# A spectral layer and a top-1 expert layer on one core: the order of the steps up to the main part, written anew

## The chip, the core and the metric

The kernel runs on one core of a Trainium2 chip. The metric is the device time of one execution in microseconds (us), the median of several runs. Engines are named as in the profile: PE does matmuls, PEld is its weight loading, DVE, ACT and POOL are the elementwise engines, SP only issues transfers. Indirect DMAs (gathers and scatters) are issued from POOL.

## The reference, cut to what matters

```python
X = np.fft.rfft(x, axis=1)                       # x: 8 x 1856 x 256
Yr = Xr @ w_r - Xi @ w_i + b_r
Yi = Xr @ w_i + Xi @ w_r + b_i
Yr = np.sign(Yr) * np.maximum(np.abs(Yr) - 0.01, 0.0)   # Yi likewise
y = np.fft.irfft(Yr + 1j * Yi, n=1856, axis=1)   # its 14848 rows go to the experts
g_idx = np.argmax(x @ w_group, axis=1)           # 4 groups
e_idx = np.argmax(xg @ w_expert[g], axis=1)      # 4 experts in each
h = np.maximum(xg[mask_e] @ w1[g, e], 0.0)       # 256 -> 1024
ye = h @ w2[g, e]                                # 1024 -> 256
out[tok_idx] = g_w * e_w * ye                    # product of both softmax values
```

Every row goes through one of 16 experts. So the rows have to be routed (a softmax and an argmax over groups, then over the experts of that group) and sorted by expert before the expert matmuls can take them in blocks.

## The kernel before

The sequences are worked on in 4 pairs. Each pair's transform is made of small steps, and so is all that follows. A step is a Python generator's piece up to its next `yield`; it issues the instructions of mostly one engine. Each kind of step has a letter: `e` is the second forward transform (PE, L760), `h` the low part of its result (DVE, L782), `y` and `k` the complex linear layer (PE, L824 and L827, then L842), `z` its share from DVE (L832) between the two, `q` the low part of its input (POOL, L808), `r` and `v` the inverse transform (PE, L866 and L884), `x` its turn (DVE, L905), `G` and `H` the gate's logits (PE, L916, and DVE, L925).

A pair's rows are routed and sorted in two halves, so there are 8 halves, here numbered first to eighth. For each half:

- `R`, 30 steps, is the route: a chain on DVE (L176 to L255) with softmax exponentials on ACT, row numbers on POOL (L218), two matmuls that count the rows per expert (L228 and L230, into a tile `bank` of PSUM), then `runs` on POOL (L236 to L240), `first_run` on DVE (L241) and the place of every row, of which L250 reads the two counts out of `bank` again.
- `S`, 11 steps, is the sort: `at`, `to` and `step` on POOL (L265 to L277), the goal on DVE (L279 to L283), `run` and `place` on POOL (L286 to L291), and then twice, for each part of the half, `in_run` (L298, L301), `here` (L304, L306) and `what` (L309), all on POOL.
- `N`, 3 steps, is PE's side of it: L325 for each part, from `in_run` and `what`, and L331 for both. `O` copies the results out (ACT, L340).
- `P` scatters the sorted row numbers into the list `lst` in DRAM (POOL, L346).

`in_run`, `here` and `what` have one buffer each, so the second part's L298 waits for the first part's L325. The pool of `bank` has 3 buffers and serves nearly all matmuls of the head: a step that takes a bank waits until the step that had it has been read out.

Once enough rows are sorted, 8 early expert jobs run beside the rest of the head, from a list a and a list b: `I` reads the list (SP, L956 and L959), `Z` converts it (POOL, L353 to L358), `F` gathers rows (POOL, L542, two gathers a step), `T` turns them (PE, L981), `U` and `D` are the two expert matmuls (PE, L1002; L1025 and L1027), `J` adds the halves (DVE, L1043) and `K` stores the rows by an indirect DMA (POOL, L624). `M` at the end gathers the first rows of the main part, which begins with L560 and L577 at about 491 us and has an order of its own.

What sets the order in the head is the string `ORDER` alone, 1702 letters: the loop at L1099 calls `next()` on the step that each letter names. Every engine runs its own instructions in the order in which the string issues them; between engines there are only the semaphores for data and for buffers. An engine that waits holds up all that stands behind it in its queue, DMAs on POOL's queue too.

Of the kernel before, what the change touches and what calls it, by code (L numbers as in the profile page):

```python
# [43 lines left out]


ORDER = """
ccQddccQdQddddjdcccddddddcddQejQffhheQiigegfcyhQQQQyfzikzhiggddkmpomcjoqcfdyjfzhiyzhkkiddggemocpdmoqdjfjlcyydfzhizkhgimk
gdpdemeofhcoqfjdjiyyzhkzgklimgdepomjofhjiqcdyzyfkhzigkgpqmdmoojfjchefiyyzkhizggdpmdkmojefofjqhyhyzzigikgpmqokfjehfyihzke
gimgpojmofhqyzjfihgykizmgpkmfoojqrsfjyyshhiziggrsskmpzrkeomfqfssohrhjsyijiyggcsdcvzwdxklwcxdmdddczvpvddqxkowwxxcmvjddlww
xywxxwecffozjdhGhdiiggHRvvpRxcwRRxxRyRwqdRkzRwxkRdvwmmRovRwxxjRxcowRReRwxyjyRzRfRkzwRRRdmhkdiRoRRigRgRGRjmfehpqRoyHRRRRR  # L50
zjfSShfyhiRzSkiggRRSRkmRpmqeojoefRfyjhyzRighkiRzSRRRRRkeRSmgpRRfRoRRqjShyigzRigmRpqoRfkjmfhNORyfojShhSSryzigigRpskmsrRzk
SmoNOjsqsrosjseyfhzNOfyilzhRrsksiPmggkvompwxxoqejwvwjvfxyxywwfzxvkwzkhmhxwxxiwcdlodgmijgGpoRSSSSSSSNOvHRqxRwvxRxSSSjcwdd
yywRzRRxvewRfxRzfRcddkwhhwkimiRxRgRRglSNOvcxwxweRRRRpmdqodfRolhfGRRjNORihjyRziRRgykgzRHRpkPmmefRofqRRRRoRhRcjdhjicRSSSRy
yzgRzRSkiddRkmgSpeRdmoqSfSfRocRjhlRNOjiRchygyRzidzgdpdkkdmqRomeRjffRRSoyRRRzhRSRhjiRgiSkemRffgRoRyrSjhhiizggNOksrymsojNO
ysRzsRPrsskmezfrohfjhsskWimgWiyloWWgzvvwxxxjwwVwvxxkevVymoVwVjyzfwRSSSSSSSfhkzxNOSShiwxmxSiwogkgmefSfjohhigNOGviygwHvNOR
xRRRxRwRzRxPRwjxRvwRwkmRxRoRjRwRexWIRRvywyWzRxRRkRWRmzRxRRRRRRlkomfGhiiojjRSSSSZygHgRzRRykRRRfFweRVmffheWzkRohRRRjhyziRm
iRgoRjSkgRRfSyTRRfRhziSRkhNOSmojmRRVRygiogjyzRzkRSSRmSRRoVkmNOoXrYsVrsRFsNOPsUrlAUsBsrWUssVWWAVvwRSSSSSSxSvxvwNOxSBwSxUx
vwwwxVwTDxxwXAYGHBSvWWwWRSxNOAvWxRRRURRBxRVRADRUwNOPwRvlxwBRRAUwIZxBRRARRvFUFDDxVVWWRRxVWRAVEBBwVEVRwDwxDJRWRRRRKRDRRRTE
DXYFEURJKJUATBlSSSAUJBWUGAASBFVXYHSTSWDSUBDANOWRWSVRKWUARVSBURBRSlRDRRRRVRRDUXEATAYSVRDRFBRUBVJERRWVWRVDRKWJNONORRERARBU
URRRAPDBFAUKRRRBDWXVYDlUABUAJTVABBDDEEKUAUBWJDDWAXYUBWVVWAEJUKKJADEBVBRSSSSSSSNOSSSJDDUTSNOEVJUAXDYABUNOAPBDBDUUAAKEKBBU  # L60
DDAJBDEEKKLDDKJMJKEJKK
"""

_OFF = {}
# [1424 lines left out]
```

## Time and profile before

| | us |
|---|---|
| median of 3 runs | 1113.06 (1109.84 to 1118.94) |
| the profiled execution | 1116.01 |
| its span | 1114.2 |
| PE busy in the span | 1047.2 (94%) |
| DVE busy | 675.2 (61%) |
| ACT busy | 489.9 (44%) |
| POOL busy | 426.5 (38%) |

The profiled execution is 2.95 us above the median, and 1.8 us of it lie around the span. Its mean granted clock of PE is 0.98 of full speed. How to read it: PE's share of 94% is a mean over a head in which it waits at many places and a main part in which it nearly doesn't; so the times by stretch matter more than the shares. An engine's idle time counts only where the chain of waits goes through it.

### The profile page before, as it was taken

How to read it: one execution, taken by the hardware profiler on the slowest of the kernel's cores; microseconds unless marked ns; L12 is line 12 of the kernel's file. 1: busy time of each engine (PE TensorE's matmuls, PEld its weight loads, DVE VectorE, ACT ScalarE, POOL GpSimd, SP SyncE). 2: the span in 40 equal slices, each digit the busy share in tenths (PEclk: the TensorE clock that was granted, in tenths of full speed). 3: DMA queues.
4: the chain of work that ended last, by engine and by line, in shares of the span. 5: the costliest groups of instructions: out<-in, count | busy, mean ns of one | idle time of the engine just before them, and what ended most of it. 6: DMA issues, size and time to landing. Idle time of an engine off the chain costs nothing.

```text
span 1114.2 us, 24634 instructions
## 1 busy us (share of the span) xinstructions
PE 1047.2 (94%) x9688; PEld 908.8 (82%) x9688; DVE 675.2 (61%) x1599; ACT 489.9 (44%) x1273; POOL 426.5 (38%) x599
## 2 busy tenths in 40 slices
PE   8899989979888889799999999999999999999996
PEld 4685767756665678789899999999999999999996
DVE  6779988989688656336544564546545455545532
ACT  2464555544533423224443553435535445444532
POOL 0121163453356264564334333434334433432422
PEclk9999989999999989899999999999999999999999
DMA  9802502421303422022313321313223233133110
GB/s 382 192 3 87 218 2 78 154 78 59 116 30 110 166 91 77 6 84 103 120 43 124 126 100 50 132 37 125 75 80 129 58 110 117 55 112 111 43 35 28
DMA packets 35047, 107.08 MB, mean 96 GB/s; under 512 B 13628, under 2 KB 16153, under 8 KB 28402
## 3 DMA queue, kind: packets, MB, share of 16 engines
q1 hardware_dynamic: 18130, 57.75, 15.7%
q0 software_dynamic: 11904, 30.74, 8.6%
q10 hardware_dynamic: 4896, 17.01, 3.9%
q8 instruction: 77, 1.26, 0.5%
q14 instruction: 40, 0.33, 0.1%
HBM read 71.34 MB, written 34.28 MB: 95 GB/s over the span
## 4 chain that ended last, share of the span: by engine, by line
PE 74%; DVE 13%; issue 5%; POOL 4%; DMA 2%; ACT 1%; POOLq 0%; SPq 0%; ACTq 0%; DVEq 0%
PE ph L577 25%; PE py L650 13%; PE py L651 6%; PE py L672 6%; PE pw L842 5%; PE bank L866 3%; PE pw L824 2%; PE pg L560 2%; PE bank L760 2%; PE ph L1002 2%; DVE big L438 2%; PE bank L916 2%; DVE yt L905 2%; PE bank L434 2%; PE bank L884 1%
## 5 line engine op out<-in xcount | busy, mean ns | idle before, releaser
L577 PE MATMUL ph<-xth,big 128*128 128x256 f32 (+8 forms) x1280 | 293.7, 313 | 2.5 <-DVE hl L584 1.6
L584 DVE SCALAR_TENSOR_TENSOR hl<-ph,hh 128x256 fp32r<-128x256 f32 (+8 forms) x528 | 169.1, 356 | 113.1 <-ACT hh L582 98.0
L577 PEld LDWEIGHTS ph<-xth,big 128*128 128x128 f32 x1280 | 218.7, 190 | 5.8 <-PE ph L577 2.2
L650 PE MATMUL py<-big,hh 128*128 128x512 f32 (+2 forms) x608 | 218.9, 400 | 0.0
L582 ACT ACTIVATE hh<-ph 128x256 fp32r<-128x256 f32 (+8 forms) x528 | 153.4, 338 | 106.9 <-PE ph L577 94.4
L577 PE MATMUL ph<-xtl,big 128*128 128x256 f32 (+8 forms) x640 | 199.2, 311 | 0.4 <-DVE xtl L565 0.4
L542 POOL DMA_INDIRECT xg<-ys_d,gi_r x92 | 91.3, 993 | 246.6 <-PE pg L560 227.4
L651 PE MATMUL py<-big,hl 128*128 128x256 f32 (+2 forms) x608 | 171.3, 282 | 0.0
L650 PEld LDWEIGHTS py<-big,hh 128*128 128x128 f32 (+2 forms) x608 | 113.0, 186 | 27.0 <-DVE yo L691 0.3
L624 POOL DMA_INDIRECT out_dram<-yo,si_r x92 | 91.6, 996 | 91.5 <-DVE yo L656 39.6
L577 PEld LDWEIGHTS ph<-xtl,big 128*128 128x128 f32 x640 | 121.6, 190 | 0.7 <-DVE xtl L565 0.6
L651 PEld LDWEIGHTS py<-big,hl 128*128 128x128 f32 (+2 forms) x608 | 113.3, 186 | 0.5 <-issue 0.3
L656 DVE SCALAR_TENSOR_TENSOR yo<-py,ent_r,yo 128x256 f32<-128x256 f32 (+1 forms) x66 | 31.9, 484 | 133.5 <-ACT yo L655 118.7
L655 ACT ACTIVATE yo<-py,ent_r 128x256 f32<-128x256 f32 (+1 forms) x66 | 31.3, 474 | 149.0 <-PE py L651 85.8
L672 PE MATMUL py<-hh,big 128*128 128x320 f32 (+4 forms) x320 | 75.4, 315 | 0.0
L808 POOL TENSOR_TENSOR xdl<-xd,xdh 128x512 fp32r<-128x512 f32 (+1 forms) x23 | 28.1, 1221 | 116.6 <-ACT xdh L801 88.2
L524 DVE TENSOR_TENSOR big<-xt,big 128x512 fp32r<-128x512 f32 x104 | 71.2, 684 | 1.0 <-ACT big L523 0.2
L842 PE MATMUL pw<-wh,xh 128*128 128x256 f32 x240 | 66.5, 299 | 5.0 <-DVE pw L832 4.9
L523 ACT CAST big<-xt 128x512 fp32r<-128x512 f32 x104 | 65.5, 630 | 0.0
L842 PE MATMUL pw<-wl,xh 128*128 128x256 f32 x240 | 62.4, 282 | 0.0
L847 ACT ACTIVATE big<-pw,nlam 128x512 f32<-128x512 f32 x60 | 41.3, 688 | 41.5 <-PE pw L842 40.0
L842 PEld LDWEIGHTS pw<-wh,xh 128*128 128x128 f32 x240 | 45.5, 190 | 15.9 <-DVE pw L832 8.5
(247 smaller groups left out, 2024.5 us busy)
## 6 DMA issues: line engine op xcount, KB each, us to landing
xt<-in_w_dram SPq DMA_DIRECT2D x34, 1024.0 KB
ys_d<-ysb ACTq DMA_DIRECT2D x32, 512.0 KB
big<-in_x_dram SPq DMA_DIRECT2D x8, 1024.0 KB
xt<-in_x_dram SPq DMA_DIRECT2D x8, 1024.0 KB
lst<-L SPq DMA_DIRECT2D x1, 1936.0 KB
xg<-ys_d,gi_r POOLq DMA_INDIRECT x92
out_dram<-yo,si_r POOLq DMA_INDIRECT x92
CI<-in_cst_dram SPq DMA_DIRECT2D x1, 1088.0 KB
```

What stands on the lines that cost most here:

```text
L523: nc.scalar.copy(out=wt[:, 2 * i, cs], in_=raws[i][:, cs])
L524: nc.vector.tensor_tensor(out=wt[:, 2 * i + 1, cs], in0=raws[i][:, cs], in1=wt[:, 2 * i, cs].bitcast(F32), op=ALU.subtract)
L542: ins = nc.gpsimd.indirect_dma_start(out=xg[0:m, c, :], out_offset=None, in_=ys_d[0:rows, :], in_offset=bass.IndirectOffsetOnAxis(ap=ids.g ...
L577: nc.tensor.matmul(o[:, :n], lhsT=a_[:, ch, fs], rhs=b_[:, ch, 0:n], start=k == 0, stop=k == 5)
L582: nc.scalar.activation(out=hh[:, f, cs], in_=o[:, cs], func=AF.Relu)
L584: nc.vector.scalar_tensor_tensor(out=hl[:, f, cs], in0=o[:, cs], scalar=0.0, in1=hh[:, f, cs].bitcast(F32), op0=ALU.max, op1=ALU.subtract)
L624: ins = nc.gpsimd.indirect_dma_start(out=out, out_offset=bass.IndirectOffsetOnAxis(ap=ids.si[0:ids.rows(t), t:t + 1], axis=0), in_=ysb, in ...
L650: nc.tensor.matmul(o, lhsT=hh[:, f, ts], rhs=w2b[:, :, f, :], start=f == 0, stop=f == 7, skip_group_check=True)
L651: nc.tensor.matmul(o[:, 0:D], lhsT=hl[:, f, ts], rhs=w2h[:, f, :], start=False, stop=f == 7, skip_group_check=True)
L672: nc.tensor.matmul(o, lhsT=w_[:, f, ds_], rhs=h_[:, f, 0:n], start=f == 0 and h_ is hh and w_ is w2h, stop=f == 7 and h_ is hh and w_ is n ...
L842: ins = nc.tensor.matmul(y, lhsT=a_[:, h, k % 2, j], rhs=t[:, j, h], start=False, stop=a_ is xl and h == 1, skip_group_check=True)
L847: nc.scalar.activation(out=z_of(pr)[:, k], in_=psum["m", pr, k], func=AF.Relu, bias=nlam)
```

## The change

The string `ORDER` is replaced by another one with the same number of each letter. Steps, tiles, buffers and the main part are the same lines as before. Of its 15 lines the first one before and the first one now are:

```diff
 ORDER = """
-ccQddccQdQddddjdcccddddddcddQejQffhheQiigegfcyhQQQQyfzikzhiggddkmpomcjoqcfdyjfzhiyzhkkiddggemocpdmoqdjfjlcyydfzhizkhgimk
...
+cdcjdcddQdcjcdddddcdQdQcddcddQeiQeiggcQQfhfyQhyeQQzkfizfighmdiihgdokgpcmqejofgjdyfypzdikgzhhkimmocgopjqefjdhyizydkzfmhko
...
 """
```

What it moves shows on the engines. First PE at the fourth half's sort matmuls, L325 twice and L331. `what` and `in_run` come from POOL; the other rows are steps of the transform. Before:

```order
L325 MATMUL bank<-in_run,what 64x80 x8
...
L842 MATMUL pw<-wh,xl 128x256 x2
L760 MATMUL bank<-T,big 64x2x32 x32
L325 MATMUL bank<-in_run,what 64x80 x8
L916 MATMUL bank<-yt,wg 64x256 x32
L884 MATMUL bank<-big,CI 64x256 x8
L827 MATMUL pw<-wc,xd 128x256 x2
L884 MATMUL bank<-big,CI 64x256 x8
L331 MATMUL bank<-K,by_place 80x64 x2
```

Now, the first piece with the first L325, the second with the other two:

```order
L325 MATMUL bank<-in_run,what 64x80 x8
L827 MATMUL pw<-wc,xd 128x256 x2
L760 MATMUL bank<-T,big 64x2x32 x32
L916 MATMUL bank<-yt,wg 64x256 x32
L884 MATMUL bank<-big,CI 64x256 x8
L827 MATMUL pw<-wc,xd 128x256 x2
...
L760 MATMUL bank<-T,big 64x2x32 x32
L884 MATMUL bank<-big,CI 64x256 x8
L325 MATMUL bank<-in_run,what 64x80 x8
L827 MATMUL pw<-wc,xd 128x256 x4
L331 MATMUL bank<-K,by_place 80x64 x2
```

Before, two `k` steps (L842, the lines left out are theirs) and one `e` step (L760) stand between the two L325. Now the gate's L916, parts of `v` (L884), of `y` (L827) and two `e` steps stand there, and four `k` steps where the second piece has its line of dots.

Second, PE at the first turn of rows gathered from list b (L981), near the seventh half's route matmuls. Before:

```order
L228 LDWEIGHTS sl
L228 MATMUL bank<-oh,sl 128x256
L230 LDWEIGHTS ones
L230 MATMUL bank<-oh,ones 128x256
L1025 MATMUL bank<-big,hh 128x512
L1027 MATMUL bank<-big,hl 128x256
L1025 MATMUL bank<-big,hh 128x512
L1027 MATMUL bank<-big,hl 128x256
...
L981 MATMUL bank<-K,xg 128x128 x4
```

Now:

```order
L1025 MATMUL bank<-big,hh 128x512
L1027 MATMUL bank<-big,hl 128x256
L981 MATMUL bank<-K,xg 128x128 x4
L1025 MATMUL bank<-big,hh 128x512
L1027 MATMUL bank<-big,hl 128x256
...
L1002 MATMUL ph<-xth,big 128x256
L228 LDWEIGHTS sl
L228 MATMUL bank<-oh,sl 128x256
```

The turn stood behind the route matmuls of that half and now stands before them, with one `D` step (four pairs of L1025 and L1027) and one `U` step (L1002) between.

Third, POOL at the last half, where the second route (`runs`, `first_run`) and the sort (from L265 on) meet the stores of the expert jobs (L624). Before:

```order
L238 TENSOR_SCALAR runs<-runs 128x16
L240 MEMSET first_run 128x1
L346 DMA lst<-by_run,goal_i 7828x64
L542 DMA xg<-ys_d,gi_b 128x256 x2
L624 DMA out_dram<-yo,si_b 16384x256 x4
L265 MEMSET at 128x1
L266 MEMSET at 128x1
L268 TENSOR_SCALAR to<-first_run 128x16
L269 TENSOR_TENSOR at<-to,base 128x16
```

Now:

```order
L624 DMA out_dram<-yo,si_b 16384x256
L298 TENSOR_TENSOR in_run<-K,run 128x640
L301 TENSOR_SCALAR in_run<-in_run 128x640
L304 TENSOR_TENSOR here<-K,place 128x256
L306 TENSOR_SCALAR here<-here 128x256
L236 TENSOR_SCALAR runs<-cnt 128x16
...
L309 TENSOR_TENSOR what<-here,ent 128x512
L624 DMA out_dram<-yo,si_b 16384x256 x2
L265 MEMSET at 128x1
L266 MEMSET at 128x1
```

Four stores stood between `first_run` and the sort of the last half; now the last `what` of the seventh half and two stores do, while the eighth half's `runs` stands behind four sort operations of the seventh.

## Rows read from the trace of the kernel before

**Rows 1.** Stretches: us, length; busy (instructions) PE, PEld, DVE, ACT, POOL; clock; DMA; GB/s
```profile
0.00:134.00 134.00, 124.14 (x1854) 90.53 (x1858) 107.50 (x204) 65.94 (x139) 17.02 (x22) 0.97 0.54 180
134.00:167.00 33.00, 27.71 (x446) 22.04 (x444) 26.50 (x69) 16.25 (x38) 20.37 (x35) 0.90 0.04 14
...
215.00:253.00 38.00, 30.58 (x464) 23.41 (x463) 31.45 (x80) 16.56 (x41) 19.41 (x34) 1.00 0.22 78
253.00:286.00 33.00, 29.25 (x483) 21.23 (x485) 27.38 (x46) 16.86 (x37) 14.36 (x22) 0.98 0.17 66
286.00:375.00 89.00, 77.43 (x976) 55.23 (x976) 66.96 (x144) 36.47 (x82) 37.96 (x64) 0.97 0.25 85
375.00:398.00 23.00, 16.93 (x104) 14.11 (x105) 14.40 (x33) 7.95 (x17) 11.34 (x22) 0.85 0.60 203
...
450.00:470.00 20.00, 14.99 (x111) 13.34 (x111) 6.70 (x14) 3.48 (x9) 14.60 (x19) 0.83 0.02 8
470.00:491.00 21.00, 18.97 (x123) 16.31 (x122) 6.34 (x12) 5.69 (x12) 10.53 (x15) 1.00 0.18 52
491.00:1114.20 623.20, 610.95 (x3924) 574.94 (x3924) 314.83 (x857) 275.29 (x805) 233.80 (x304) 0.99 0.27 87
sum 1114.20, PE 1047.19 PEld 908.77 DVE 675.15 ACT 489.92 POOL 426.55; mean PE 95.20 PEld 82.62 DVE 61.38 ACT 44.54 POOL 38.78
```

**Rows 2.** Waits of PE, 0 to 491 us: total, times, longest
```profile
PE bank L325 <- POOL what L309: 11.8, 4, 5.0
PE bank L981 <- DVE t L250: 6.0, 1, 6.0
PE pw L842 <- DVE pw L832: 4.9, 8, 1.1
...
PE bank L325 <- DVE xl L782: 3.4, 1, 3.4
PE bank L228 <- DVE oh L222: 2.2, 1, 2.2
PE bank L916 <- DVE t L250: 1.8, 1, 1.8
```

**Rows 3.** Chain of waits, fourth half's sort: start, us, what
```profile
278.64 1.61 PE pw L842 x12
280.25 1.16 PE bank L760 x64
...
283.48 1.05 POOL what L309
```

**Rows 4.** Chain of waits, list b
```profile
372.66 0.28 PE bank L331 x4
...
389.15 0.94 POOL xg L542
...
392.65 0.43 DVE t L250
...
393.13 1.11 PE bank L981 x4
```

**Rows 5.** Timeline of POOL, last half: start, us, instruction, [idle before]
```profile
448.81 0.98 POOL L624 DMA_INDIRECT out_dram<-yo,si_b  x1 [8.72 <-DVE yo L1043]
...
453.41 1.26 POOL L298 TENSOR_TENSOR in_run<-K,run 128x640 f32<-128x640 f32 x1
454.75 2.14 POOL L301 TENSOR_SCALAR in_run<-in_run 128x640 f32<-128x640 f32 x1
...
458.86 1.05 POOL L309 TENSOR_TENSOR what<-here,ent 128x512 f32<-128x512 f32 x1
461.39 1.26 POOL L298 TENSOR_TENSOR in_run<-K,run 128x640 f32<-128x640 f32 x1 [1.48 <-PE bank L325]
...
466.15 1.05 POOL L309 TENSOR_TENSOR what<-here,ent 128x512 f32<-128x512 f32 x1
```

**Rows 6.** Line L301, all 16: duration in ns min/median/max
```profile
L301 POOL TENSOR_SCALAR in_run<-in_run x16: 1807/1822/2137, 146.5 to 462.7; 128x640 f32<-128x640 f32 x16
```

**Rows 7.** Waits of DVE, 0 to 491 us: total, times, longest
```profile
DVE first_run L241 <- POOL first_run L240: 12.1, 8, 5.2
```

More of the change, by code (lines that the diff above doesn't have):

```diff
@@ L46 @@
 ORDER = """
-ccQddccQdQddddjdcccddddddcddQejQffhheQiigegfcyhQQQQyfzikzhiggddkmpomcjoqcfdyjfzhiyzhkkiddggemocpdmoqdjfjlcyydfzhizkhgimk
-gdpdemeofhcoqfjdjiyyzhkzgklimgdepomjofhjiqcdyzyfkhzigkgpqmdmoojfjchefiyyzkhizggdpmdkmojefofjqhyhyzzigikgpmqokfjehfyihzke
-gimgpojmofhqyzjfihgykizmgpkmfoojqrsfjyyshhiziggrsskmpzrkeomfqfssohrhjsyijiyggcsdcvzwdxklwcxdmdddczvpvddqxkowwxxcmvjddlww
-xywxxwecffozjdhGhdiiggHRvvpRxcwRRxxRyRwqdRkzRwxkRdvwmmRovRwxxjRxcowRReRwxyjyRzRfRkzwRRRdmhkdiRoRRigRgRGRjmfehpqRoyHRRRRR
@@ L51 @@
[L51 to L60, printed above, removed]
@@ L61 @@
-DDAJBDEEKKLDDKJMJKEJKK
+cdcjdcddQdcjcdddddcdQdQcddcddQeiQeiggcQQfhfyQhyeQQzkfizfighmdiihgdokgpcqmejofgjdyfypzdikgzhhkimmocgopjqefjdyhizydkzfmhko
+cmqjgeodjyfdlyzzicgfkhmddhpigqkmoiocgjfedjfyzyphzkkqhicdgmmoejoidgfjyzykzpdhmcoqdjdkfmyiheizfkihgojggpiyzgmeopfjhkmqyizf
+foigqeijgpikgmfyhhzqoghkfjmhyzojrksysrfzfmohhsskjplyrzmosskjrmeoqssyicvfzihdjfhgygwkwpxvmdvwxxcqwxodczdwxjydwlkvxdxmewcx
+wffodiGzghdivgwhHjRRRkxRywmeRvRpwxRzqRoRjRxwckiiyxRdmgdgvzopffqjlckRxRwdhxywdRmzRRvRhReoiRRxRkjgycwxmzowjRRddigkRfRmypzf
@@ new lines @@
+GqkRojlymeRiRSRHRSSihochzdRjdykfSRzRhRgRgeRmSfopqSijhikRgyRSRmeRgzRkRfpfNqiohShjgRmiOoygSfhRRrfzjhpsRSkRsmrRoRsRyjqyzsRS
+zrNOsskRRRrRkmsojmeRNfiysoiOzgvfxvwwkgpjxhhxwmxvwwoxjeRwvxxqwixywgiyfRSRcSdgdGhzSSfhHvRxvpSwRSzRxwcSRdRRqkRwkmdmRexRxNRo
+RowfvRjjyylxRziRgwiRSRxwRRfShRkPOvShwzekRxmRgwRxSoiRRmjRlfRoGRpjqRHfhhyyRRSzzcdgcRdRikmlgRdkmpeiRodocifcqdjdygzRjdSyzkkf
+hNmmhogpRjdccOoqReSjdRddfyzRyigdigpkRSzehfRSRNqmRiRikojOyRmgeRRfgfihRzoShkRShijRNygRmRSOoffPrjhzhgsSSRskRRlyzRSmrsRkrsNo
+RmjsRSsyzOreiSRoSjkssffhyzNOigWvkhwSmxgovSxwWxwjwSWlvmSxxxvNyxxSVOwRewfVoiSVwGwfhhHzvjRxwyRzWRRSkxRiVlgRRkmoeRgwmofjiSjv
@@ new lines @@
+wNRRxyyOxwiRzWRNvOggWzRxkfxRmkhRhwmRRvRojeojwyyxRRRwzRPfPxzRwfkiRRkgRimRRRmSeIiigoSZRSGohjjShSHyfWyRzRSkgRRzRkhfRSmehmRg
+NoRojRjRFySzfhWfykiiRzkRVRmRRgRTORgoSRhjRRSymRoSRRzkRRRmFNOoVrRXYUVsVsRrSssUArBUsASBRrWSslSWSsSUsSANTONXVPWWVvYxOSwwSvvx
+SBWVvxAUwBUxwSxwWwxNwvxOwNxROAVBGVHxWlAUvRwwVPxwWwVRvwBRRxwvUxwWDRARIDZRREWDRRxDxxRVDBARFxBRWFRRRwRJDRTEDXVYUFURJVARRABR
+KRlTBEDRURAURVRAGBXRYUARWBSEBHRRUDABSJDWVUAVKFERJRURWRBlRTXJTRASBYRRRDDRRFERRRSJRUARWRUSBDSUARKRBKKAUXDBWVRSEDWNVKAYBSRO
+RVSDEJWWUAUSDRARDEBUJlTBVSRNKUWVARKRSBAWSFSXBDVYDESWJUSSWOUSDVNAVJAOBNOPBTSUDSUXDEASSDYVWABNVJRBKKKOUANOUVBPURDAEBDAJEUD
@@ L62 @@
+ADLDBBDKDJEDMKJEKEJJKK
 """
```

## The prediction

> **What bounds the kernel now.** I read the table of stretches first [rows 1]. PE is the busiest engine in every stretch, and from 491 us on, in the main part, it works 610.95 of 623.20 us with instructions that the change doesn't touch. So only the head, 0 to 491 us, is in play. PE's 1047.19 us of work less the main part's 610.95 leave 436.24 in those 491: 54.8 us idle. The reader is also to see the clock column: 0.90, 0.85 and 0.83 in the three stretches 134 to 167, 375 to 398 and 450 to 470, and 0.97 to 1 in the others shown. One minus that, times the length, is what runs at the lower level of 1.2 GHz costs there: 3.3 + 3.5 + 3.4 = 10.2 us; with 4.0 in the first stretch and 3.4 in 253 to 286 and 286 to 375 the head loses some 17 us so. Each of the three stretches holds one of the longest PE waits, so the low clock is read as the price of a PE that has stood still.
>
> Next, who ended PE's waits [rows 2]. The largest group is L325, the matmuls of the sort, held by `what` of L309 on POOL: 11.8 us in 4 waits. Then one wait of 6.0 us by L981 (the turn of gathered rows), put down to the route's DVE chain; one of 3.4 us by L325 for DVE's L782; one of 2.2 us by L228. Four places, and the rest of the idle time is crumbs of about 1 us.
>
> Last, the chain of waits at three of these places.
> The fourth half's second L325 [rows 3]: behind the first L325 PE has only 1.61 us of L842 and 1.16 us of L760, 2.8 us together, while POOL needs a whole part of the sort for the next `what`. Such a part took 5.8 us in the last half, from L298 at 461.39 to the end of L309 at 467.20 [rows 5]. 2.8 against 5.8 is the wait of 3 us.
> List b [rows 4]: L331 ends at 372.94; the fourth gather's issue starts at 389.15; only then does POOL reach `runs` of L236, DVE ends L250 at 393.08 (392.65 + 0.43), and L981 starts at 393.13. The bank that L981 needs is released by that chain of the route, because L228 and L230 stand before L981.
> The last half [rows 5]: POOL stands 8.72 us before the last of four stores, for DVE's L1043; only then, at 449.8 (448.81 + 0.98), does its sort begin. `what` is ready at 459.91, and the longest of L325's waits, 5.0 us, ends there [rows 2, 5].
>
> **The change part by part.** No instruction is added or removed. Every cost is a cover: how much work stands on PE between the producer's start and the consumer. I added up the mean duration of what stands between, on PE and on the producing chain, at each place where PE takes something from another engine. For before this gives shortages of 55.8 us over 63 places, beside 54.8 us of idle time measured [rows 1]; so the tally may be used for the new order, where it gives 12.4 us over 20 places.
>
> Sort matmuls. Between the first and second L325 of the fourth half, PE now has 12.5 us of work in place of 2.8, against 5.8 needed; in the fifth half 7.7 in place of 4.9; in the others 7 to 26. POOL's sort steps begin right behind the route's last step and no longer stand in one block before the matmuls. From these 253 to 286 gets 3.5 of its 3.75 us back, 215 to 253 gets 5 of its 7.42 (2.9 of the L325 wait, and half of the rest), and 134 to 167 gets 3 of 5.29 (the wait of 3.4 for L782, whose bank another step takes now) [rows 1, 2].
>
> Route matmuls. The waits for L222 (2.2) and L250 (1.8, before L916 of the sixth half) lie in 286 to 375: 3 of its 11.57 us [rows 1, 2].
>
> List b. PE now has L981 before L228 of the seventh half, so its bank doesn't wait for the route any more. What is left is the gather: L981 can't start before the rows land. That landing has no row; the four gathers are issued one behind the other, some 0.95 us each, and L981 started at 393.1, so it lies between 386 and 393.1; I take 391, a microsecond behind the end of the last issue at 390.1 [rows 4]. That is 18 us after L331, and PE has 19.0 us of work there now (13.1 before). Of 6.0 us I take 5. With the landing at 386 the whole 6.0 go; with 393.1 the cover is 1.2 us short (20.2 against 19.0), and 4.8 go.
>
> Last half. The sort starts behind two stores and not behind four, so the 8.72 us don't stand in front of it. From the second route matmul to the first L325 PE has 19.7 us (26.2 before), for a chain of about 19. I take 3.5 of 5.0, as the margin is under 1 us; 470 to 491 gives 0.5 [rows 1, 5].
>
> 0 to 134, 167 to 215, 398 to 450 and the main part: 0. The transform's matmuls there wait for DMA and for crumbs, and covers are alike.
>
> Sum of idle time removed: 3 + 5 + 3.5 + 3 + 5 + 3.5 + 0.5 = 23.5 us.
>
> The clock: with the waits of the three stretches gone, most of their 10.2 us comes back; I take 9, since not all of each wait goes. The lower end is 0 (another wait keeps the clock down), the upper end 17 (all the head loses).
>
> New short covers: 12.4 us, of which 2.4 stand in the old order too (the head's first transforms), so +10. These are places where a step now stands closer: L325's second matmul group in the seventh half, the route's L228 steps of three halves (about 1 us each), and L241 on DVE, which stands behind the sort steps on POOL. The ends for this term are 0, if the slack carried over from earlier steps fills them, and 22: each of the 20 places costing 1.1 us, the longest wait of L842 for DVE [rows 2].
>
> Sum: −23.5 − 9 + 10 = −22.5. The profiled execution took 1116.0 us, so 1093.5; it lies 2.95 above the median of the runs, so on the median's scale 1090.5, given as 1091. With every term at its good end it is −23.5 − 17 + 0 = −40.5, so 1072.6; at its bad end −23.5 + 22 = −1.5, so 1111.6.
>
> One rule bears on this. The in_run comparison of L301 took 1.81 us at least, 1.82 in the median and 2.14 at most [rows 6]; the 2.14 stands in the first part of the last half's sort [rows 5]. The Trainium skill, "GPSIMD Engine Reference", section "1. Specifications", says that this engine shares its SBUF interfaces with VectorE, with contention when VectorE runs a two-port mode or reads two SBUF inputs. So sort steps spread beside DVE work would get longer by it. The trace agrees in the sign at most: the median lies at the low end although DVE was busy four fifths of the stretches from 134 to 375. By the rule every part of a sort would take the 0.3 us more, and the sum would be 1 us higher for the four places with thin cover; by the rows it stays.
>
> **Rivals.** Their times are on the median's scale, 2.95 below the sum with the profiled execution.
> 1. Waits move to DVE. DVE works 152.3 of 193 us in the four stretches shown from 134 to 375 [rows 1], in the order of the string; a PE wait for POOL may become a PE wait for DVE. Then only the waits that stand apart from the transforms go: 5 + 3.5 + 0.5, and the clock stays as it is elsewhere. −9 in all, so 1104. For it: L842 waits for DVE's L832 already, 8 times [rows 2]. Against it: DVE has the same work and PE has more of its own work between.
> 2. Nearly all goes: no new short cover bites and the crumbs shrink too. From 134 to 491 idle is 44.9 us (54.8 less 9.86 of the first stretch) [rows 1]; if 27 of it go, three fifths, and 13 of the 17 us of clock, −40: 1073.
> 3. The clock doesn't return although the waits go, since the new crumbs keep PE as uneven: −23.5 + 10 = −13.5: 1100.
> 4. Slower: DVE in the queue behind POOL. DVE's L241 waits for POOL's L240, now 12.1 us in 8 waits, the longest 5.2 [rows 7]. In the new order `runs` (L236 to L240) stands behind sort steps or stores in seven of eight halves, and in the last one behind stores that wait for L1043. DVE stands in L241, and behind it every transform or expert step. If each of eight times DVE stands for a whole part of the sort, 6.5 us as the longer one in the last half, 453.41 to 459.91 [rows 5], that is 52 in place of 12, and one store of 8.72 on top: +48.6 [rows 5, 7], against 32.5 removed: +16, so 1132 by the profiled execution and 1129 by the median. It turns to a loss from about 4 us more per half on, 5.6 in place of 1.5. For it: the last half's rows in the order. Against it: in six of the halves it stood behind sort steps in the old order as well.
>
> **How the numbers follow.** Forecast 0.55 at 1091, own range 1083 to 1099; rival 1 0.17 at 1104; rival 2 0.12 at 1073; rival 3 0.08 at 1100; rival 4 0.08 at 1129. A measurement of this kernel tells about 1% from no change; 1% of 1113.06 is 11.1 us, so faster means under 1101.9. Faster: 0.55 + 0.12 + 0.08 = 0.75; same: 0.17; slower: 0.08. The range goes from one end of the sum to the other, 1072 to 1112; it holds the times of rivals 1 to 3 and leaves out rival 4 and the outer parts of rivals 1 and 2.
>
> **What would show it.** Right: L325 waits for L309 fall from 11.8 us to under 3; L981's wait of 6.0 is gone or put down to a gather and under 1; the main part starts near 468 us and lasts 623 as before; clock over 0.95 at the places of the three low stretches. Wrong: DVE's wait at L241 over 30 us (rival 4), L842's waits for L832 well above now (rival 1), or a head as short but a clock still under 0.9 (rival 3). The forecast falls altogether if PE idle up to the main part is still above 45 us.

## The result and the profile after

The new order takes 1069.39 us in the median of 4 runs (1068.39 to 1071.51), the kernel before 1114.05 (1109.84 to 1118.94) beside it. The ratio is 0.9586, with a 95% interval of 0.9551 to 0.9621: 4.1% faster. The forecast was 1091 with a range of 1072 to 1112. The direction was right; the gain of 44.7 us is twice the 22 that were forecast, and the time lies 2.6 us below the range.

The profiled execution took 1071.51 us, its span is 1069.7. The table of stretches shows the head (up to the main part's first matmul, L560) and the main part, and below the dots the head again, cut at 134 us and up to 448.0; the columns are those of [rows 1]:

```profile
0.00:448.20 448.20, 424.19 (x5761) 330.90 (x5762) 360.49 (x740) 211.30 (x467) 194.68 (x296) 0.99 0.34 117
448.20:1069.70 621.50, 609.23 (x3930) 572.47 (x3928) 315.27 (x859) 275.65 (x806) 232.30 (x303) 1.00 0.27 88
...
0.00:134.00 134.00, 122.17 (x1860) 90.85 (x1863) 102.82 (x197) 63.93 (x139) 18.32 (x23) 0.97 0.51 169
134.00:448.00 314.00, 301.81 (x3914) 239.89 (x3906) 257.67 (x544) 147.37 (x328) 176.36 (x273) 0.99 0.27 95
```

The same cut of before, at its first L560:

```profile
0.00:488.80 488.80, 435.41 (x5761) 333.48 (x5761) 359.81 (x740) 213.61 (x467) 190.90 (x294) 0.97 0.32 107
488.80:1114.20 625.40, 611.77 (x3928) 575.29 (x3928) 315.34 (x859) 276.31 (x806) 235.65 (x305) 0.99 0.27 88
```

Here the 44.5 us between the two spans can be taken apart by subtraction alone. The head is 40.6 shorter, for the same 5761 matmuls on PE. PE's idle time in it went from 53.4 (488.80 less 435.41) to 24.0: 29.4 us. Its busy time went from 435.4 to 424.2, 11.2 us for the same matmuls: that is the clock, 0.97 before and 0.99 now (one minus the clock, times the length, is 14.7 and 4.5, so about 10 by the rounded rows). The main part is 3.9 us shorter, with no edit in it.

PE's waits in the head now (total, times, longest), answering to [rows 2]:

```profile
PE bank L760 <- issue: 4.2, 1, 4.2
PE pw L842 <- DVE pw L832: 2.9, 6, 1.2
PE bank L325 <- POOL what L309: 2.4, 1, 2.4
PE bank L434 <- DMA big<-in_x_dram: 2.1, 4, 0.7
PE ph L1002 <- DVE hl L1013: 2.0, 2, 1.6
...
PE bank L981 <- DMA xg<-ys_d,gi_b: 0.8, 1, 0.8
```

L325's waits for L309 fell from 11.8 us to 2.4, its wait of 3.4 for L782 is gone, L981's 6.0 is 0.8 and is put down to the gather, and the waits of L228 and L916 don't appear any more. The one wait for L309 that is left lies in the last half, and a low clock stands behind it (0.83):

```profile
415.00:425.00 10.00, 7.63 (x59) 7.05 (x58) 2.55 (x4) 1.55 (x5) 9.37 (x9) 0.83 0.01 3
425.00:448.20 23.20, 23.20 (x167) 20.98 (x166) 8.60 (x15) 6.95 (x15) 13.16 (x18) 1.00 0.17 47
```

The chain of waits shows what stood in front of it: on POOL two gathers stand among the sort's steps, from 409.33 to 411.64, and L301, the sort's longest operation, has its longest duration. That these two made the wait wasn't tried by itself.

```profile
409.33 1.05 POOL xg L542
...
410.68 0.96 POOL xg L542
...
413.65 1.68 POOL in_run L298
...
415.40 2.15 POOL in_run L301
...
419.15 1.06 POOL what L309
...
420.25 1.15 PE bank L325 x16
```

And the wait that the rival on the slower side was about, DVE's L241 behind POOL [rows 7], is as it was:

```profile
DVE first_run L241 <- POOL first_run L240: 12.0, 8, 4.8
```

### The profile page after: what moved, and what is told of

Read it like the earlier page. It is cut to its first block, busy times and chain, and to the rows that moved or that the text cites. A ratio compares the mean times of both kernels' runs of the same rounds, so it can differ in the third digit from the quotient of the medians.

```text
span 1069.7 us, 24651 instructions
## 1 busy us (share of the span) xinstructions
PE 1033.4 (97%) x9688; PEld 903.4 (84%) x9688; DVE 675.8 (63%) x1599; ACT 486.9 (46%) x1273; POOL 427.0 (40%) x599
## 3 DMA queue, kind: packets, MB, share of 16 engines
q8 instruction: 77, 1.26, 0.5%
## 4 chain that ended last, share of the span: by engine, by line
PE 78%; DVE 11%; issue 4%; POOL 3%; DMA 2%; ACT 2%; ACTq 0%; POOLq 0%; SPq 0%; DVEq 0%
PE ph L577 26%; PE py L650 13%; PE py L651 7%; PE py L672 6%; PE pw L842 5%; PE ph L1002 3%; PE pw L824 2%; PE pg L560 2%; PE bank L884 2%; PE bank L866 2%; PE bank L760 2%; DMA big<-in_x_dram 2%; PE bank L434 2%; PE bank L916 2%; PE bank L1025 1%
## 5 line engine op out<-in xcount | busy, mean ns | idle before, releaser
L624 POOL DMA_INDIRECT out_dram<-yo,si_r x92 | 91.5, 995 | 94.0 <-DVE yo L656 43.1
L842 PE MATMUL pw<-wh,xh 128*128 128x256 f32 x240 | 66.9, 301 | 2.9 <-DVE pw L832 2.9
L842 PE MATMUL pw<-wl,xh 128*128 128x256 f32 x240 | 62.2, 281 | 0.0
L842 PEld LDWEIGHTS pw<-wh,xh 128*128 128x128 f32 x240 | 45.4, 189 | 17.7 <-DVE pw L832 7.6
```

The source lines that it names most:

```text
L624: ins = nc.gpsimd.indirect_dma_start(out=out, out_offset=bass.IndirectOffsetOnAxis(ap=ids.si[0:ids.rows(t), t:t + 1], axis=0), in_=ysb, in ...
L842: ins = nc.tensor.matmul(y, lhsT=a_[:, h, k % 2, j], rhs=t[:, j, h], start=False, stop=a_ is xl and h == 1, skip_group_check=True)
```

## The experiments

Since the loop takes any order that keeps each step's inputs, most experiments are strings too. Each ratio is against runs of the kernel before on the same chip; a percent is 11 us.

**Two halves of the string.** Is the gain made place by place, or does the early part build up a lead that the late part spends? One string has the new order up to the first list read of the expert jobs and all other steps in the order of before, the other one the reverse:

```python
n = new.index("I")                    # about 290 us in the new order, 300 in the old
ab = new[:n] + steps of old that are not in new[:n], in old's order
ba = old[:m] + steps of new that are not in old[:m], in new's order
```

> The new order up to the first list read of the expert jobs, all steps that are left in the order of before. Theory 1 (gains are local: each PE wait that is covered gives back itself and the low clock behind it): by the two traces PE is idle 30.1 us up to the first turn of list a before and 16.3 us with the new order, and the low clock costs 8.5 and 3.4 there, so about -19 us against before (1095). Theory 2 (the gain comes from a lead that the early part builds up and the late part spends): the late waits shrink too without being re-ordered, -30 or more. Theory 3 (the late part eats it, since its waits are for lists and stores that are no earlier): -8 or less.

> The old order up to the first list read, all that is left in the new order. Theory 1 (local): idle after the first turn of list a 23.3 us before and 7.7 with the new order, the low clock behind it 8.5 and 1.7, and 4 us in the main part: -22 to -26 us (about 1090), and together with the run that has the halves the other way round about the whole -44.7. Theory 2 (lead from the early part): -12 or less, as the late part has no lead to spend. Theory 3: -35 or more.

Measured: 0.983 (0.9795 to 0.9865), 1089.86 against 1109.04, so 19 us; and 0.9773 (0.9743 to 0.9803), 1084.79, so 24 us. The product of the two ratios is 0.9607, beside 0.9586 of the whole. Theory 1 holds on both, with 19 forecast and 19 measured, and 22 to 26 forecast and 24 measured: each stretch keeps what its own order gives. PE's waits from 134 us to the main part say the same. Of the first string, with the late part of before:

```profile
PE bank L981 <- DVE t L250: 6.2, 1, 6.2
PE bank L325 <- POOL what L309: 5.8, 2, 5.0
```

Of the second, with the early part of before:

```profile
PE bank L325 <- POOL what L309: 8.7, 3, 3.2
...
PE bank L325 <- DVE xl L782: 3.4, 1, 3.4
PE bank L981 <- DMA xg<-ys_d,gi_b: 2.6, 1, 2.6
```

The late waits of 6.0 and 5.0 stay as they were where the late part is the old one, and the early ones of 2.9, 3.2 and 3.4 where the early part is. Only L981 keeps 2.6 us with the new late part alone, beside 0.8 in the whole new order.

**The sort matmuls of two halves alone.** In the order of before, the third half's first L325 (`N`) and its copy (`O`) go behind a `k` step, the fourth half's second behind the gate's `G`:

```diff
-...jhlRNOjiRchygyRzidzgdpdkkdmq...fjohhigNOGviyg...
+...jhlRjiRchygyRzidzgdpdkNOkdmq...fjohhigGNOviyg...
```

> The order of before, with two sort matmul groups alone later on PE: the third half's first L325 behind one more piece of transform (13.2 us of cover become 17), the fourth half's second L325 behind the gate's L916 (2.8 become 6.4). Theory 1 (cover): the waits of 2.9 and 3.2 us for L309 go and with the second the low clock at 284 us (1.7): -6 to -8 us. Theory 2 (DVE is the bound there, so PE only waits elsewhere): 0 to -3 us, with L842's waits for L832 or L916's for L905 up by as much.

Measured: 0.9911 (0.9882 to 0.9940), 7 to 13 us. In its profile the two waits are gone, and of the others only L842's for L832 has grown by more than 0.5 us, from 3.9 to 5.1; PE's waits from 134 us to the main part:

```profile
PE bank L981 <- DVE t L250: 5.8, 1, 5.8
PE bank L325 <- POOL what L309: 5.6, 2, 5.0
PE pw L842 <- DVE pw L832: 5.1, 7, 1.1
PE bank L325 <- DVE xl L782: 3.4, 1, 3.4
```

L309 holds PE for 5.6 us in 2 waits, before it was 11.8 in 4: 6.2 us, as the two places had (2.9 and 3.2). DVE took 1.2 us of it back, theory 2's way, but is not the bound there. The clock was not what theory 1 said. Before, 0.57 was granted behind the wait at 284 us; here that stretch is at full speed, but 0.66 stands behind the next wait, that of L916 (1.8 us), which had been followed by the full clock before:

```profile
284.00:288.00 4.00, 3.42 (x40) 2.43 (x44) 0.78 (x3) 0.50 (x2) 0.53 (x1) 0.57 0.02 6
305.80:309.80 4.00, 3.97 (x66) 2.68 (x67) 3.96 (x6) 1.23 (x4) 2.50 (x7) 1.00 0.00 0
```

are the two places in the profile of before, and

```profile
278.00:282.00 4.00, 4.00 (x119) 3.07 (x122) 3.53 (x7) 3.39 (x8) 3.74 (x5) 1.00 0.34 129
299.00:304.00 5.00, 4.49 (x52) 2.96 (x56) 4.83 (x10) 1.23 (x4) 3.13 (x11) 0.66 0.01 2
```

those of this run. That the low stretch moved from one wait to the next because the first one went is not shown. A later run, whose order up to there is that of before, has in its profile a low clock behind both waits, here that of L916:

```profile
310.40:314.40 4.00, 4.00 (x44) 2.60 (x48) 3.96 (x6) 1.23 (x4) 2.53 (x7) 0.57 0.00 0
```

So the same wait at the same place of the order is followed by a low clock in one execution and not in another. The head of this profiled execution is 5.5 us shorter than before (483.3 against 488.8), about the waits alone; the medians, on one chip, differ by 7.7 us (1101.33 against 1109.04) and the ratio gives 9.9, and where the rest lies isn't shown, as before was not profiled on that chip.

**The last half's sort ahead of the stores.** First the seven sort steps go forward, past three of the four stores:

```diff
-...FAUKRRRBDWXVYDl...EJUKKJADEBVBRSSSSSSSNOSSS...
+...FAUKRRRSSSSSSSBDWXVYDl...EJUKKJADEBVBRNOSSS...
```

> The order of before, with the first seven sort steps of the last half ahead of three of the four stores on POOL, PE's order untouched. Theory 1 (POOL stands for a store and the sort behind it): the wait of 5.0 us before L325 goes and the low clock behind it (3.4): -7 to -9 us. Theory 2 (the wait only moves: the second L325 has 5.0 us of cover for 5.8, and the stores come later and hold the expert jobs' buffers): -2 to -4 us with a new PE wait of 2 us or more, and the low clock stays.

Measured: 0.9975 (0.9955 to 0.9995): between nothing and 5 us. Theory 2 was right that the gain goes elsewhere, and the timeline of DVE says where, better than that theory did:

```profile
433.86 0.60 DVE L255 TENSOR_REDUCE slot<-t 128x16 f32<-128x256 f32 x1
437.81 0.24 DVE L279 SCALAR_TENSOR_TENSOR step<-first_run,K,step 128x17 f32<-128x17 f32 x1 [3.35 <-POOL step L277]
```

The second sort step is DVE's (L279). It had come forward with the others, and DVE stood in it for 3.35 us until POOL was through with L277; behind it in DVE's queue stood L1013, on which PE's L1002 waits. PE's waits from 430 us on were then

```profile
PE ph L1002 <- DVE hl L1013: 2.3, 3, 1.2
PE bank L325 <- POOL what L309: 1.4, 1, 1.4
PE ph L1002 <- DVE xtl L990: 0.8, 1, 0.8
```

where before had 5.0 for L309 and 1.1 for L1013. A low clock came along at a place where before had 1.00:

```profile
439.00:446.00 7.00, 6.00 (x33) 5.74 (x34) 4.60 (x8) 1.56 (x3) 6.49 (x8) 0.76 0.00 0
```

So the edit was made anew, with the three stores (`K`) put behind the sort steps and all other engines left as they were:

```diff
-...BDDEEKUAUBWJDD...EJUKKJADEBVBRSSSSSSSNOSS...
+...BDDEEUAUBWJDD...EJUJADEBVBRSSSSSSSKKKNOSS...
```

> The order of before with three of the four stores behind the last half's first seven sort steps on POOL; DVE, ACT and PE keep their order. In the run with the sort steps moved forward, DVE's own step of the sort (L279) came forward with them and stood 3.4 us for POOL's L277, and PE's L1002 waited behind it; that gave 0.9975. Theory 1 (that stand of DVE ate the gain): without it the wait of 5.0 us for L309 goes and the low clock behind it, 1.4 us return at the second L325, so -5 to -7 us, 0.994 to 0.9955. Theory 2 (the second L325, or the stores that come later, hold the end anyway): -3 us or less, 0.9975 or above, with new waits at L1002, L1025 or L560.

Measured: 0.9918 (0.9892 to 0.9945), 6 to 12 us; 1099.05 against 1108.37. The wait of 5.0 us for L309 became one of 1.1, and the stretch whose clock was 0.83 [rows 1] runs at full speed:

```profile
450.00:470.00 20.00, 18.87 (x156) 17.22 (x155) 9.59 (x17) 7.42 (x16) 10.67 (x11) 1.00 0.06 21
```

Theory 1's mechanism holds: the late start of the sort was worth what the two losses add up to, or somewhat more than the 5 to 7 us expected, and with DVE's stand in the first try a third to a half of that was left. The two ratios come from two chips, and the profiled execution here is the longest of the six (1106.58), with low clocks in the unchanged part (the row of 310 us above). A stretch that leaves both out goes from the turn of list b to the main part. It takes 95.7 us before (393.13 to 488.78), 92.4 in the first form (393.27 to 485.66) and 89.2 in the second (398.62 to 487.80): 3.3 us less, and 6.5.

**List b's turn ahead of the route.** `T` moves ahead of the seventh half's L228, and a `J`, which frees the bank that the route then takes, with it:

```diff
-...DJRWRRRRKRDRRRTEDXYFEURJKJUA...
+...DJRWTJRRRRKRDRRREDXYFEURKJUA...
```

> The order of before, with the first turn of list b (L981) ahead of the seventh half's route matmuls on PE, and with it the step of the expert job (L1043) that frees the bank for the route. Theory 1 (the cover counts): L981 meets its gather, which lands some 18 us after L331, with 13 us of PE work in front, so 4 to 5 of the 6.0 us stay, and the low clock stays: -1 to -3 us. Theory 2 (the route's chain in front of the bank was the whole wait): the 6.0 us go and 3.4 of clock: -8 to -10.

Measured: 1.0006 (0.9981 to 1.0032), no difference. The wait has the same length and another name:

```profile
391.88 1.09 PE L981 MATMUL bank<-K,xg 128*128 128x128 f32 x4 [5.79 <-DMA xg<-ys_d,gi_b]
```

Here L331 ends at 373.73:

```profile
373.45 0.28 PE bank L331 x4
```

The rows of the gather are there 18.2 us later (391.88), and in [rows 4] the route's chain ends 20.2 us behind L331 (372.94 to 393.13): two ends 2 us apart, and where the turn waits for both the profile names the later one. Theory 2 is out; theory 1's 1 to 3 us lie within the interval at most in part. The place ahead of the route alone gives nothing with 13 us of PE work in front of the turn; in the new order 19 us stand there and 0.8 us of wait is left. So the work in front counts; that it would do without the new place wasn't tried.

**Those places together** (the two sort matmuls, the first form of the last half, list b).

> The order of before with four places alone changed: the two sort matmul groups, the last half's sort ahead of three stores, list b's turn ahead of the route. Theory 1 (the named places add up): the two runs already made gave -9.9 and -2.8, list b some -2 more: -14 to -16. Theory 2 (a wait that goes lets a later one shrink or grow): outside -10 to -20. Either way 25 us or more of the 44.7 would stay with the rest of the order.

Measured: 0.9909 (0.9876 to 0.9942), 10.1 us beside 9.9 + 2.8 − 0.7 = 12.0 of the single runs; they add up within the intervals. The 14 to 16 expected were missed, since list b gave nothing. Some 35 of the 44.7 us come from what the string does beyond these edits, at these places too (list b's cover, the last half's stores); they are split by the two halves above, not place by place.

**One wait put back into the new order.** The fourth half's second L325 goes forward to stand behind one `e` step, with the POOL steps that it needs:

```diff
-...yxxSVOwRewfVoiSVwGwfhhHzvj...RRSkxR...fjiSjvwNRRxyyOxw...
+...yxxSSSSVOwReNwfVoiVwGwfhhHzOvj...RRkxR...fjijvwRRxyyxw...
```

> The new order, with the fourth half's second L325 drawn forward behind one transform step, so that it has 1.9 us of cover for a POOL part of 5.8. Theory 1 (each place pays for itself, and for the clock behind it): a wait of 3.5 to 4 us for L309 returns, and 1.7 us of low clock, +5 to +6 us. Theory 2 (the order behind has slack, and a PE that comes later waits less there): the wait returns, other waits shrink by half of it or more, and the time grows by 2 us or less.

Measured: 0.9645 (0.9600 to 0.9690) beside 0.9586 of the new order, so about 6.6 us more, though each is against its own runs of before and the intervals overlap. The trace is sharper, in PE's timeline

```profile
270.65 1.34 PE L325 MATMUL bank<-in_run,what 128*64 128x80 f32 x16 [4.63 <-POOL what L309]
```

and in the table of stretches:

```profile
266.00:272.70 6.70, 2.07 (x27) 1.65 (x28) 3.34 (x5) 2.93 (x7) 5.66 (x6) 0.74 0.40 159
```

A wait of 4.63 us is back, and a low clock with it, where the new order has PE busy without a break at full clock:

```profile
262.00:276.00 14.00, 14.00 (x243) 10.66 (x242) 13.33 (x27) 10.08 (x22) 7.65 (x7) 1.00 0.39 154
```

The other waits behind it stayed: L842 for L832 2.3 us in 5 waits and L1002 for L1013 2.1 in 2, and L325 in the last half 2.6 (7.2 less 4.6). From the first L325 of that half to the main part it takes 190.7 us (263.06 to 453.71) where the new order takes 182.4 (265.77 to 448.19): 8.2 us, about what 4.6 of wait and 3.4 of low clock (0.57 from 268.2 to 276.2) add up to. Theory 1 holds, with more than its 5 to 6: a place pays for itself and for the clock behind it, and no slack behind it took up any of this.

**What is left in the new order.** Two waits were taken on: that of 2.4 us in the last half, by putting its first L325 one turn and one expert step later; and the 4.2 us near 45 us, in the middle of a transform step, where the trace names no releaser ("issue") and the DMA engines are nearly full (0.99):

```profile
46.00:48.00 2.00, 0.00 (x0) 0.00 (x0) 0.00 (x0) 0.00 (x0) 0.00 (x0) 1.00 0.99 336
```

The kernel before has 3.6 us of the same kind there. The first of L727's loads was made to wait for a matmul; `last_e`, left out here, is the last L760 issued before it:

```diff
 x_in[pr, dc] = t = xp.tile([128, 32, 64], F32, name="xt")
-nc.sync.dma_start(out=t, in_=x_v[pr, dc])
+ins = nc.sync.dma_start(out=t, in_=x_v[pr, dc])
+if (pr, dc) == (2, 0):
+    tc.add_manual_dep(ins.ins, last_e[-1].ins.name, landed, reason="...")
```

They ran first together, then all apart on one chip, with the new order beside them.

> The new order, and two things more: the last half's first L325 stands one turn and one expert step (2 us) later, and the first of the loads that fill the DMA engines while PE stands 4.2 us in the middle of a transform step near 45 us goes behind a later transform step (L727 waits for the last L760 issued before it). Theory 1 (PE stands there because its instructions come by DMA behind that load): the 4.2 us shrink to under 1.5 and the low clock behind it (3.4) goes, and the 2.4 us before L325 go with 1.7 of clock: -6 to -10 us against the new order. Theory 2 (the instructions come late whatever the load): the 4.2 and 3.4 stay, and only L325's part goes: -2 to -4.

Measured: 0.9537 (0.9492 to 0.9581), some 5.5 us under the new order's 0.9586 and so between the two theories (6 to 10, and 2 to 4); in its trace PE's wait without a releaser near 45 us is gone, as theory 1 had it.

> The new order once more, beside three variants of it on one chip. All theories: 0.9586 of before, within its interval (0.955 to 0.962). Its idle time up to the main part, 24.0 us in the first profile, should change only where the loads of the start are in play (the 4.2 us near 45 us), if that wait is one of instructions that come late by DMA.

> The new order with the last half's first L325 alone one turn and one expert step (2 us) later. Theory 1 (cover): the wait of 2.4 us goes and 1.7 of low clock behind it, -2 to -4 us against the new order. Theory 2 (the end of the head is set by the chain from the last L331 to the first gather of the main part, and this chain is later by the 2 us): 0.

> The new order with the one load alone behind a later transform step. Theory 1: the wait in the middle of a transform step near 45 us is gone (under 0.5), -3 to -6 us against the new order, with the clock behind it. Theory 2 (that wait differs from execution to execution, and the load has nothing to do with it): 0 to -1 in the median of the runs.

> The new order with both. The two lie 370 us apart: the sum of the two runs above, -5 to -8 us against the new order, if gains are local; less than the larger one alone if the end of the head is held by something else.

| | us, median of 6 | ratio to before, interval |
|---|---|---|
| the new order | 1065.52 | 0.9582 (0.9552 to 0.9612) |
| L325 later | 1063.51 | 0.9563 (0.9532 to 0.9593) |
| load later | 1061.64 | 0.9550 (0.9521 to 0.9580) |
| both | 1059.83 | 0.9528 (0.9499 to 0.9557) |

By the medians −2.0, −3.9 and −5.7: what theory 1 said of each, and the sum of the two. The intervals against before overlap, but each of the six runs with the load later (up to 1063.87) and with both (up to 1060.60) is below all six of the new order (from 1064.14); of L325 alone (1060.70 to 1065.57) this can't be said. The load's place shows in the stretch from 40 to 52 us, here of the new order on the same chip,

```profile
40.00:52.00 12.00, 9.49 (x118) 6.86 (x117) 6.09 (x12) 3.40 (x7) 0.00 (x0) 0.86 0.68 183
```

and here with the load later:

```profile
40.00:52.00 12.00, 12.00 (x196) 9.62 (x199) 9.11 (x18) 6.13 (x14) 1.28 (x1) 1.00 0.46 165
```

PE is busy without a break, at full clock. That the time of this load decides over this wait is shown; that PE's own instructions come by the DMA engines and stood behind it is what the profile of before suggests (a queue "q8 instruction" moves 1.26 MB), and it wasn't tried by itself. Both together beat the two kernels of this case.

## Why the prediction was wrong by half

By its own steps:

- *Only the head is in play.* Right in the main: 40.6 of 44.5 us are there. The main part's 3.9 us can't be given to the order: with a head that is mostly the order of before, the same main part took 616.7 us in the run with the two sort matmuls moved (the row below), less than in either kernel's profile. On that chip it took 616.6 to 617.1 us in four runs, whatever half of the head was new; on another one 620.2 and 620.8 behind new heads and 622.7 and 623.3 behind old ones. So it differs by chip, and whether some 2 us of it are the head's stays open.

```profile
483.30:1100.00 616.70, 607.01 (x3930) 572.42 (x3928) 316.23 (x859) 279.85 (x806) 233.43 (x304) 1.00 0.27 88
```

- *"New short covers: +10".* This is the step that failed. From 134 us on PE was idle for 44.9 us before; the forecast left 44.9 − 23.5 + 10 = 31.4 of it, and 12.2 are measured (314.0 less 301.81). The 23.5 to be removed were about right: the waits that the prediction names are 25.2 us in [rows 2] (11.8, 6.0, 3.4, 2.2 and 1.8), and 3.2 of them are left (2.4 and 0.8), so 22.0 went. It is the rest of the idle time, 44.9 − 25.2 = 19.7 us, that should have grown by 10 and fell to 12.2 − 3.2 = 9.0 (up to 1.4 us of the 19.7 lie behind L560). The tally had gone over every place of the new order. So its 12.4 us, less the 2.4 of the first transforms, were all that would be left from 134 us on, and the prediction added them to old waits that it had left in place. Used as a total, 44.9 − 10.0 = 34.9 removed and 9 of clock, it would have given 1116.0 − 43.9 − 2.95 = 1069.2. That this is the measured time almost to the digit is luck. No run shows the tally, and it is not that sharp: ahead of 134 us it has 2.4 where 9.9 us were idle before and 11.8 now, half of it or more for DMA and "issue", and from there on its 53.4 for before (55.8 less 2.4) stand beside 44.9. Its agreement with the 54.8 held for the sum alone. Which covers shrank the rest is shown for the two halves, not place by place.

- *The covers themselves.* Right where they were named. Two sort matmuls alone gave the 6.2 us of wait that they stood for, and one cover taken away cost 4.63, a little more than the 3.5 to 4 expected. List b's cover of 19.0 us left 0.8, as its rows landed 19.2 us behind L331 (340.66 to 359.84) and not 18. The last half was the one where the margin was called thin: of its 5.0 us 2.6 went and not 3.5.

- *List b.* The number was right, 5.2 of 6.0 us. But the prediction began with the bank and the route as the cause, and the run with the turn ahead of the route shows that its place alone gives nothing. Its second sentence, that what is left is the gather, was the one that counted.

- *The clock: 9 us back.* 11.2 us by PE's busy time in the head, for the same matmuls. The size was nearly right; the way to it, one low stretch for one wait, was too simple, as the waits at 284 us and of L916 show, and at the last half's place the clock is still 0.83 where over 0.95 was the sign to look for.

- *Rivals.* The second (nearly all goes, 1073) came about, with 0.12: the crumbs shrank too, as it said. The first (waits move to DVE) did not: L842's waits for L832 fell from 4.9 us to 2.9. The third did not: the clock came back. The fourth did not in the new order: DVE's L241 waits 12.0 us in place of 12.1. Its mechanism exists, though: DVE standing in its queue for a POOL step took about half of the gain or more in the first run with the last half's sort forward (0.9975 in place of 0.9918, 3.3 us in place of 6.5).

- *Contention.* The Trainium skill, "GPSIMD Engine Reference", section "1. Specifications", has POOL and DVE share their SBUF interfaces. L301 takes 1.81 us at least, 1.83 in the median and 2.15 at most with the sorts spread, as in [rows 6]. So the trace shows 0.3 us at the most, in single operations, and nothing of it is seen in the sum.

## What to carry to other kernels

Where an order written out by hand is changed, the time can be read from covers: for every place where the busiest engine takes something from another, how much work stands in front of it, and how long the producer's chain is. The shortages that the new order has are then what will be left of such waits (10.0 against 12.2 us here); they aren't added to a share of the old ones. Waits for DMA and "issue" are no covers (2.4 against 11.8 us ahead of 134). When a step is moved past others, all engines that it uses move with it: a sort brought forward gave about half of its worth or less (0.9975 against 0.9918, 3.3 against 6.5 us in the traces) as long as another engine's small step came along and stood in that engine's queue.

## What the runs showed of the hardware

Low-clock stretches were not tied to one wait. Behind the same 1.8 us wait of L916, 1.00 was granted in the profile of before and 0.57 in that of a run whose order differs only later; behind the 3.2 us wait ahead of it the clock was low in both. A wait of 4.63 us put into a stretch where PE had been busy without a break at full clock brought a low stretch with it (0.74), and the two together cost 8.2 us up to the main part. DVE's 3.35 us in L279 held up the L1013 behind it, and PE's L1002 with it. And PE can stand in the middle of a step with no other engine in sight: 3.6 us before, 2.5 and 4.2 us near 45 us in two runs of the new order, gone when one load of x was issued later.
